# Another cut of the last keys' load, and another place for reordering the last output weights, in a decode attention kernel

## Chip, cores, metric

One core of a Trainium2 chip. The time is the device time of one execution in microseconds. The trace of an execution (its length is called the span) covers some 1.8 us less than the time that is reported for it.

## The reference

Two decode attentions (4 queries) side by side, each with its projections; only the second one, B, matters here, since it streams 537 MB of the 587:

```
q = (x @ wq) as (B=4, H=32, 1, Dh=128);  k, v: (4, 32, 8192, 128) bf16
p = softmax(q k^T / sqrt(Dh));  o = p v;  out_b = o @ wo        (wo: 4096 x 512)
```

## The kernel before

B runs in 64 chunks, each two heads of one batch: 4 MB of keys, 4 MB of values, 128 tiles of 128x128 each. SyncE issues all loads in order: keys of c+1, values of c. Per chunk TensorE transposes the key tiles (groups of 8, into three PSUM tiles in turn, copied out by VectorE or ScalarE), multiplies them with q, and then runs the value matmuls of chunk c-1 with the softmax of chunk c threaded between. Pairs of chunks run in a loop on each engine. The last keys and the last values are loaded in pieces:

```python
LASTV = (64, 32, 16, 8, 8)
...
def dma_kv(kind, c):
    ...
    if kind == "k" and c == NC - 1:
        x = slice(0, NTB // 2 * P), slice(NTB // 2 * P, NTB * P)      # 64 + 64 tiles
        sch.add_dma("sp", lambda e: e.dma_start(dst[:, x[0]], src[:, x[0]]), "d_h%d" % at, waits=waits, key=(kind, c))
        sch.add_dma("sp", lambda e: e.dma_start(dst[:, x[1]], src[:, x[1]]), "d_kl", key="kl")
        return
...
# SyncE counts up when the weights of the pair, and for the last chunk the second key piece, have landed:
sch.add("sp", lambda e: e.sem_inc(sems["eng_sp"], 1), waits=[("wos", hp)] + (["kl"] if c == NC - 1 else []), ...)
...
def emit_T(s):                      # 8 transposes of group g
    ...
    if c >= NCA and c % 2 == 1 and g == NTB // TG // 2:
        waits += [("wos2", ahead(c, 2))]          # the count above
...
sch.mark()                          # after the loop
norm_sum(NC - 1)
emit_wol()                          # 4 matmuls reorder the last output weights, ScalarE and VectorE copy them out
for g in range(chunks[NC - 1]["NG"]):
    emit_pv(NC - 1, g)              # 128 value matmuls; each of the 5 pieces is waited for at its first tile
pv_done(NC - 1)
emit_fin(NC - 1)                    # output matmul, copy, store
```

## Time and profile before

| | before |
|---|---|
| time, first three runs | 1374.6 us (1374.56 to 1375.19) |
| span of the trace | 1373.7 us; its own execution took 1375.56 us |
| load queue busy | 99.7% of the span |
| TensorE (PE) busy | 86% |
| wait for the last value chunk but one, ahead of 1359.14 us | 2.1 us |
| TensorE's granted clock in the 3.41 us behind it | 0.50 |

How to read it: with the load queue busy for 99.7% of the span, I take it that the stream sets the time here, and that the engines add only what they do after its last bytes (the last value piece landed at 1368.99). The granted clock is the share of the full clock that TensorE was given. The lines are in the prediction. Where its stretches of 3.41 us begin is called the phase of the clock; free means not tied to the kernel.

### The profile page before, as it was taken

How to read it: one execution, taken by the hardware profiler on the slowest of the kernel's cores; microseconds unless marked ns; L12 is line 12 of the kernel's file. 1: busy time of each engine (PE TensorE's matmuls, PEld its weight loads, DVE VectorE, ACT ScalarE, POOL GpSimd, SP SyncE). 2: the span in 40 equal slices, each digit the busy share in tenths (PEclk: the TensorE clock that was granted, in tenths of full speed). 3: DMA queues.
4: the chain of work that ended last, by engine and by line, in shares of the span. 5: the costliest groups of instructions: out<-in, count | busy, mean ns of one | idle time of the engine just before them, and what ended most of it. 6: DMA issues, size and time to landing. Idle time of an engine off the chain costs nothing.

```text
span 1373.7 us, 59835 instructions
## 1 busy us (share of the span) xinstructions
PE 1184.8 (86%) x27000; PEld 1134.7 (83%) x27001; DVE 656.5 (48%) x1434; ACT 434.8 (32%) x650; POOL 7.3 (1%) x28
## 2 busy tenths in 40 slices
PE   4898899888889988888889888988888888888988
PEld 4787799888878888888889878988888888888987
DVE  1675455444444544444445444544444444444543
ACT  1553233233323332232333323332332233223332
POOL 2000000000000000000000000000000000000000
PEclk9899999999999999999999999999999999999999
DMA  9999999999999999999999999999999999999998
GB/s 401 423 424 433 426 434 426 437 429 433 429 433 429 432 429 434 428 434 428 434 428 434 429 435 431 431 431 431 431 431 432 430 432 430 432 430 432 430 427 338
DMA packets 25253, 587.53 MB, mean 428 GB/s; under 512 B 2816, under 2 KB 2832, under 8 KB 6288
## 3 DMA queue, kind: packets, MB, share of 16 engines
q1 hardware_dynamic: 25208, 587.22, 99.7%
q8 instruction: 16, 0.26, 0.1%
q14 instruction: 5, 0.04, 0.0%
q10 hardware_dynamic: 24, 0.01, 0.0%
HBM read 587.21 MB, written 0.01 MB: 427 GB/s over the span
## 4 chain that ended last, share of the span: by engine, by line
DMA 59%; PE 37%; DVE 2%; issue 1%; ACT 1%; SPq 0%; DVEq 0%
DMA kv<-in_B_k_cache_dram 54%; PE tr L406 22%; PE sc L408 9%; PE po L408 3%; DMA kv<-in_B_v_cache_dram 2%; DMA kv<-in_B_wq_dram 2%; PE fin L408 2%; DMA kv<-in_A_k_cache_dram 1%; PE ms L408 1%; DVE sA L525 1%; ACT kt L474 0%; DVE rm L534 0%; ACT pba L595 0%; DVE sA L523 0%; PE ms L406 0%
## 5 line engine op out<-in xcount | busy, mean ns | idle before, releaser
L406 PE MATMUL tr<-identb,kv 128*128 128x128 bf16 x8704 | 696.7, 230 | 138.1 <-DMA kv<-in_B_k_cache_dram 133.2
L476 DVE COPY kt<-tr 128x1024 bf16<-128x1024 bf16 x736 | 502.4, 691 | 457.7 <-PE tr L406 453.1
L406 PEld LDWEIGHTS tr<-identb,kv 128*128 128x128 bf16 x8704 | 550.9, 104 | 160.3 <-DMA kv<-in_B_k_cache_dram 91.5
L474 ACT ACTIVATE kt<-tr 128x1024 bf16<-128x1024 bf16 x352 | 359.3, 1023 | 664.9 <-PE tr L406 664.7
L408 PE MATMUL sc<-qb,kt 128*128 128x64 bf16 x8704 | 448.8, 196 | 14.5 <-ACT kt L474 12.8
L408 PEld LDWEIGHTS sc<-qb,kt 128*128 128x128 bf16 x8704 | 368.9, 101 | 25.8 <-ACT kt L474 20.2
L408 PE MATMUL po<-pbb,kv 128*128 128x64 bf16 x8320 | 285.6, 192 | 6.9 <-issue 4.9
L408 PEld LDWEIGHTS po<-pbb,kv 128*128 128x128 bf16 x8320 | 264.8, 97 | 9.3 <-issue 5.1
L575 ACT ACTIVATE pbb<-sc,negb 64x128 bf16<-64x128 f32 x128 | 51.5, 403 | 257.6 <-DVE negb L562 256.9
L539 DVE TENSOR_REDUCE rm<-sc 64x1 f32<-64x128 f32 x128 | 37.0, 289 | 58.9 <-PE sc L408 58.0
L551 DVE TENSOR_REDUCE gm<-ms 1x2 f32<-1x128 f32 (+1 forms) x72 | 20.1, 279 | 48.5 <-PE ms L406 48.5
L562 DVE COPY negb<-ms 128x1 f32<-128x1 f32 (+1 forms) x72 | 11.4, 159 | 47.1 <-PE ms L408 47.1
L408 PE MATMUL ms<-identf,gx 1*128 1x1 f32 (+1 forms) x144 | 27.4, 257 | 0.8 <-DVE zA L681 0.8
L664 DVE TENSOR_TENSOR oz<-po,rz 128x8 bf16<-128x8 f32 x33 | 5.5, 167 | 41.5 <-PE po L408 41.5
L408 PEld LDWEIGHTS ms<-identf,gx 1*128 1x128 f32 (+1 forms) x144 | 21.2, 184 | 4.8 <-DVE zA L681 0.9
L575 ACT ACTIVATION_READ_ACCUMULATOR pbb<-sc,negb 64x1 f32 x128 | 23.7, 185 | 0.0
L406 PE MATMUL ms<-identf,rm 128*1 128x128 f32 (+1 forms) x72 | 19.7, 274 | 4.1 <-DVE rm L534 4.1
L408 PE MATMUL po<-pba,kv 128*128 128x64 bf16 x512 | 20.5, 199 | 2.8 <-issue 1.5
L408 PEld LDWEIGHTS po<-pba,kv 128*128 128x128 bf16 x512 | 17.9, 102 | 5.4 <-ACT pba L595 4.2
L408 PE MATMUL fin<-wos,zB 128*4 128x512 bf16 x64 | 19.0, 378 | 0.0
L555 DVE TENSOR_SCALAR gx<-gm 1x128 f32<-1x128 f32 (+1 forms) x72 | 15.9, 221 | 2.5
L681 DVE CAST zB<-ms 64x8 bf16<-64x8 f32 x64 | 10.5, 164 | 9.4 <-PE ms L408 8.9
(61 smaller groups left out, 169.7 us busy)
## 6 DMA issues: line engine op xcount, KB each, us to landing
kv<-in_B_k_cache_dram SPq DMA_DIRECT2D x63, 4096.0 KB, 26.8
kv<-in_B_v_cache_dram SPq DMA_DIRECT2D x63, 4096.0 KB, 31.2
kv<-in_A_k_cache_dram SPq DMA_DIRECT2D x8, 2048.0 KB, 12.7
kv<-in_A_v_cache_dram SPq DMA_DIRECT2D x8, 2048.0 KB, 14.4
kv<-in_A_wq_dram SPq DMA_DIRECT2D x1, 4096.0 KB, 12.3
kv<-in_B_wq_dram SPq DMA_DIRECT2D x1, 4096.0 KB, 27.2
wor<-in_A_wo_dram SPq DMA_DIRECT2D x8, 512.0 KB, 9.1
wos<-in_B_wo_dram SPq DMA_DIRECT2D x16, 256.0 KB, 20.4
```

What stands on the lines that cost most here:

```text
L406: sch.add("pe", lambda e: e.transpose(o, l, r), waits, key)
L408: sch.add("pe", lambda e: e.matmul(o, l, r, start=start, stop=stop), waits, key)
L474: sch.add("act", lambda e: e.activation(dst, src, ACTF.Copy), waits=waits, key=("ev", s))
L476: sch.add("dve", lambda e: e.tensor_copy(dst, src), waits=waits, key=("ev", s))
L525: emit = lambda e, src=src, b=b: e.scalar_tensor_tensor(out=t, in0=src, scalar=mk[:, b:b + 1], in1=t, op0=ALU.mult, op1=ALU.add)
L539: sch.add("dve", lambda e, src=src, pp=pp: e.tensor_reduce(out=rm[pp, m, 0:1], in_=src, axis=AX.X, op=ALU.max), waits=[("S", ch["s_last"]) ...
L551: sch.add("dve", lambda e: e.tensor_reduce(out=gm[0:C, m, 0:U], in_=src, axis=AX.X, op=ALU.max), waits=[("trm", c)], key=("gmax", c))
L555: sch.add("dve", lambda e: e.tensor_scalar(out=dst, in0=gv, scalar1=-scale, scalar2=None, op0=ALU.mult), waits=[("gmax", c)], key=("gx", c))
L562: sch.add("dve", lambda e: e.tensor_copy(negb[:, m, 0:C], ms[:, col:col + C]), waits=[("bc", c)], key=("negb", c))
L575: sch.add("act", lambda e, src=src, pp=pp, n=n, u=u: e.activation(probs_of(c)[pp, :, u], src, ACTF.Exp, bias=negb[pp, m, 0:1], scale=scale ...
L664: sch.add("dve", lambda e: e.tensor_tensor(out=o, in0=i0, in1=i1, op=ALU.mult), waits=waits, key=("oT", c))
L681: sch.add("dve", lambda e, src=src, pp=pp: e.tensor_copy(z[pp, :].rearrange("p (r b) -> p r b", r=k), src), waits=[("sm", c)] + free if h ...
```

## The change

The intent, as I read it, was to cut the keys so that less work is left behind their last landing, and to use a pause between value pieces for the reordering. Core of the diff:

```diff
+LASTK = 96
-                x = slice(0, NTB // 2 * P), slice(NTB // 2 * P, NTB * P)
+                x = slice(0, LASTK * P), slice(LASTK * P, NTB * P)
-                    if c >= NCA and c % 2 == 1 and g == NTB // TG // 2:
+                    if c >= NCA and c % 2 == 1 and g == LASTK // TG:
                         waits += [("wos2", ahead(c, 2))]
         norm_sum(NC - 1)
-        emit_wol()
         for g in range(chunks[NC - 1]["NG"]):
             emit_pv(NC - 1, g)
+            if g == LASTV[0] // TG - 1:
+                emit_wol()
```

## The prediction

> **What bounds the kernel now.** I read the page first, for the bound of the whole. Its header, engine shares, the three rows of slices and the row of the load queue:
>
> ```profile
> span 1373.7 us, 59835 instructions
> PE 1184.8 (86%) x27000; PEld 1134.7 (83%) x27001; DVE 656.5 (48%) x1434; ACT 434.8 (32%) x650; POOL 7.3 (1%) x28
> DMA  9999999999999999999999999999999999999998
> q1 hardware_dynamic: 25208, 587.22, 99.7%
> ```
>
> The load queue is busy for 99.7% of the span, at 427 GB/s, from the first slice to the last but one. So 587 MB through a full queue set the time, and no saving on an engine in the middle counts. The change touches the last two chunks only (and the place of one wait inside the loop), so I then read the chain of waits over the last 50 us (start, length, what):
>
> ```profile
> 1328.78 30.31 DMA kv<-in_B_v_cache_dram
> 1359.09 0.05 issue
> 1359.14 0.65 PE po L408 x16
> ...
> 1365.36 0.31 PE ms L408 x2
> 1365.68 0.07 issue
> 1365.75 0.81 PE tr L408 x3
> 1366.56 3.76 PE po L408 x128
> ...
> 1371.27 0.68 DVE outsb L716
> ```
>
> The last thing that the chain takes from the queue is the value chunk before the last, landed at 1359.09. From there on it is TensorE alone: the values of that chunk with the last scores between them, the sum (ms), the reordered weights (tr, line 408), the 128 value matmuls of the last chunk, output. Ahead of 1359.14 the list of TensorE's waits has one wait of 2.1 us for that value chunk. Third, the issues of the last key halves in SyncE's timeline, and their time to landing from the views of the two lines (369 and 370):
>
> ```profile
> 1323.43 0.33 SPq L369 DMA_DIRECT2D kv<-in_B_k_cache_dram  x1
> 1323.81 0.43 SPq L370 DMA_DIRECT2D kv<-in_B_k_cache_dram  x1
> DMA to landing us min/median/max: 21.0/21.0/21.0
> DMA to landing us min/median/max: 25.6/25.6/25.6
> ```
>
> The halves land at 1344.4 and 1349.4: 4.9 to 5.0 us for 2 MB, so 2.45 us for 1 MB. TensorE starts on the last keys at 1345.15, directly after the values before them (their last matmul ends at 1345.3): the first half is only 0.7 us early. Last, the busy time of TensorE and its granted clock in stretches of 3.41 us (length, PE, PEld, DVE, ACT, POOL, clock, DMA share, GB/s):
>
> ```profile
> 1352.81:1356.22 3.41, 3.41 (x78) 3.33 (x78) 1.50 (x3) 1.65 (x2) 0.00 (x0) 1.00 0.96 413
> 1356.22:1359.64 3.42, 1.16 (x34) 0.92 (x31) 0.69 (x1) 0.40 (x1) 0.00 (x0) 1.00 0.97 412
> 1359.64:1363.05 3.41, 3.41 (x67) 3.34 (x64) 1.00 (x4) 0.00 (x0) 0.00 (x0) 0.50 0.95 398
> 1363.05:1366.46 3.41, 3.34 (x73) 2.82 (x72) 0.58 (x4) 1.20 (x5) 0.00 (x0) 1.00 0.85 343
> ```
>
> This is the one line that makes the change worth anything: in the stretch with the 2.1 us wait TensorE is busy for 1.16 of 3.42 us, and the next stretch, which lies on the path to the end, runs at half clock. Through the whole trace, going by the clock records, every full-clock stretch of this length with about 1.85 us or more of idle TensorE was followed by one at half clock, and none with under 1.78 us was.
>
> [...] That the phase is free no trace here shows; I take it as a risk. [...]
>
> **The change part by part.**
>
> 1. Keys in 3 MB and 1 MB. The same bytes in the same order: everything from the end of the keys on lands as before (keys 1349.4, values 1359.1). Only the first piece is later by 1 MB, 2.45 us: 1344.4 + 2.45 = 1346.9. TensorE, ready at 1345.3, now waits 1.65 us there. The last keys took from 1345.15 to 1357.08 = 11.9 us; from 1346.95 they end at 1358.9. That is still 0.2 us ahead of 1359.09. So the 2.1 us wait is split: some 1.65 us ahead of the keys, 0.2 us behind them. The first is below the 1.8 us at which half clock followed, the second far below. Then the half-clock stretch at 1359.64 goes. What it cost is read from the same stage one chunk before, at full clock: its values ran from 1340.63 to 1345.31 = 4.68 us; the last such stage from 1359.14 to 1365.36 = 6.22 us. So 1.54 us of TensorE's path are saved.
>
> 2. The wait for the second piece. The listing of instructions shows that the wait for SyncE's count leaves the transposes of group 8 and sits on the output matmul after group 10; the wait meant for group 12 is dropped, since the same value has then been awaited. Before, group 8 began at 1350.92, 1.5 us after the landing at 1349.4, without idle. After, that matmul comes at 1352.37 + 1.8 = 1354.2, 4.8 us after it. No wait before, none after: 0. In the loop the wait moves to a later place; TensorE has 133 us of waiting for keys over the whole kernel, so one more register instruction per two chunks is 0.
>
> 3. Reordered weights between the value matmuls. Four matmuls, 0.9 us of TensorE with the gap before them (1365.68 to 1366.56), come after the first 64 value matmuls. Same work on the same engine. It saves only if a piece of the values is waited for. Before, nothing is: 128 in 3.91 us, 30.5 ns each. After, with part 1: values end at 1363.8, sum to 1364.2 (0.35); piece 1 has landed (1329.2 + 34.8 = 1364.0); 64 matmuls of 30.5 ns to 1366.15; weights to 1367.05; piece 2 (landed at 1366.5) to 1368.0; piece 3 (1367.7) to 1368.5; piece 4 (1368.3) to 1368.75; piece 5 lands at 1331.4 + 37.6 = 1369.0 and is waited for. Eight matmuls and the last one's drain, some 0.45 us: 1369.45. With the weights first, as before, the last matmuls wait for the same piece 5 and end at 1369.45 too. So this part gives 0; the copies of the weights (0.60 and 0.69 us) end by 1368.3, ahead of their use.
>
> The sum: 1370.3 - 1369.45 = 0.85 us, not 1.54, because the landing of the last value piece caps it. What follows the last value matmul (3.4 us to the end of the span) stays. So 1374.6 - 0.85 = 1373.75 if all goes as in this trace. It is 0.06%: nothing near 2%.
>
> **The rivals.**
>
> - *Nothing is gained, because the clock's phase is free.* With a 2.1 us wait, a 3.41 us window may be cut so that neither part holds 1.8 us of idle; I put it at a half at most. Timed runs of before without the half-clock stretch would already end at the cap, and after gains 0. For it: two runs at 1374.56 and 1374.60 and one at 1375.19, a spread of the very size. Against: the two lowest agree within 0.04 us. Time: 1374.6.
> - *The half clock moves instead of going.* If the new wait ahead of the keys is 1.8 us or more within one window, the keys run at half clock for 3.41 us and lose 1.7 us: they end at 1360.6, values at 1365.3, the end as before: 1374.6. A little worse in both: 1375.5. For it: 1.65 is near 1.8. Against: it must also fall whole into one window.
> - *The moved wait disturbs the loop.* Thirty-odd passes; 0.5 us each on the path would be 16 us. Against: the queue is at a share of 1.00 throughout, fed some 20 us ahead, and the wait only moves later. Time then 1380 to 1390; 1%.
> - *The reorder pays of itself*, by filling a wait for value pieces: at most 0.9 us, and only were the pieces later than the sums say. The last piece would still cap it: 1373.7, the same figure.
>
> **Range and chances.** I weigh 1373.75 at two thirds, 1374.6 at one third: 1374.0. Runs of one kernel spread by 0.6 us[...]; 1372.6 to 1375.4 should hold it 8 times in 10. Two per cent is 27 us, and no path above reaches it but a failure of the loop: 0.01 faster, 0.98 within, 0.01 slower.
>
> **What would show it.** Right: the first key piece lands some 2.4 us later, TensorE waits about 1.65 us for keys near 1345.3, the wait for the value chunk at 1359.1 falls under 0.5 us, the clock in the stretch behind it is 1.00, and the last value matmuls wait for the last piece instead of running without a gap. Step 1 is wrong if the clock is 0.50 after 1359 or in the keys; step 2 if a wait for SyncE stands in front of the output matmul; step 3 if the values end earlier than the last piece plus 0.5 us. The whole is wrong if the queue's rate in the middle, 430 to 432 GB/s, differs: then time came or went where I saw no cause.

## The result

Median 1374.43 us (1374.17 to 1374.70, 6 runs), before 1374.58 us (1374.27 to 1375.19, 6 runs). The ratio is 0.9999, 95% interval 0.9986 to 1.0012: the same.

The page after, header and load queue: the stream is as full as before.

```profile
span 1372.9 us, 59836 instructions
q1 hardware_dynamic: 25208, 587.22, 99.7%
```

TensorE's waits from 1340 to 1373 us (waited in total, times, longest), first before, then after:

```profile
PE po L408 <- DMA kv<-in_B_v_cache_dram: 2.1, 1, 2.1
```

```profile
PE tr L407 <- DMA kv<-in_B_k_cache_dram: 1.7, 1, 1.7
PE po L409 <- DMA kv<-in_B_v_cache_dram: 0.5, 2, 0.2
```

The one wait of 2.1 us has become 1.7 us for keys and two of 0.2 us for values. SyncE's two key issues, and their time to landing, after:

```profile
1322.49 0.33 SPq L370 DMA_DIRECT2D kv<-in_B_k_cache_dram  x1
1322.86 0.43 SPq L371 DMA_DIRECT2D kv<-in_B_k_cache_dram  x1
DMA to landing us min/median/max: 24.4/24.4/24.4
DMA to landing us min/median/max: 26.5/26.5/26.5
```

That is 1346.9 and 1349.4: the first piece 2.5 us later than the first half, the whole at the same time. The stretches between changes of the clock, after (columns as in the prediction):

```profile
1344.13:1347.55 3.42, 1.74 (x51) 1.62 (x48) 0.33 (x3) 0.91 (x4) 0.00 (x0) 1.00 1.03 436
1347.55:1350.96 3.41, 3.41 (x79) 3.35 (x77) 2.66 (x4) 1.35 (x2) 0.00 (x0) 1.00 1.07 456
1357.79:1361.20 3.41, 2.98 (x89) 2.73 (x86) 1.27 (x3) 0.67 (x1) 0.00 (x0) 1.00 0.94 399
1361.20:1364.62 3.42, 3.42 (x97) 3.31 (x96) 1.00 (x5) 0.91 (x4) 0.00 (x0) 1.00 0.98 404
```

The clock (third number from the right) is 1.00 in all of them: the half-clock stretch is gone. And the end of the chain of waits, after:

```profile
1330.42 38.58 DMA kv<-in_B_v_cache_dram
1369.00 0.05 issue
1369.04 0.42 PE po L409 x8
```

Before, the chain ended in 12 us of TensorE alone; now it is the load of the last value piece, landed at 1369.00, with eight matmuls behind it. The last value matmul ends 10.35 us after the landing of the value chunk at 1359.1 instead of 11.22; the span is 0.8 us shorter. So the two traces show the whole predicted gain, while the medians differ by 0.15 us, within the noise. That gap is the question for the experiments.

### The profile page after: what moved, and what is told of

Read it like the earlier page. It is cut to its first block, busy times and chain, and to the rows that moved or that the text cites. A ratio compares the mean times of both kernels' runs of the same rounds, so it can differ in the third digit from the quotient of the medians.

```text
span 1372.9 us, 59836 instructions
## 1 busy us (share of the span) xinstructions
PE 1181.3 (86%) x27001; PEld 1131.3 (82%) x27001; DVE 657.2 (48%) x1434; ACT 434.8 (32%) x650; POOL 7.3 (1%) x28
## 3 DMA queue, kind: packets, MB, share of 16 engines
q1 hardware_dynamic: 25208, 587.22, 99.7%
## 4 chain that ended last, share of the span: by engine, by line
DMA 59%; PE 37%; DVE 1%; issue 1%; ACT 1%; SPq 0%; DVEq 0%
DMA kv<-in_B_k_cache_dram 53%; PE tr L407 23%; PE sc L409 9%; DMA kv<-in_B_v_cache_dram 3%; PE po L409 2%; DMA kv<-in_B_wq_dram 2%; PE fin L409 2%; DMA kv<-in_A_k_cache_dram 1%; PE ms L409 1%; DVE sA L526 1%; ACT kt L475 0%; ACT pba L596 0%; DVE rm L535 0%; DVE sA L524 0%; PE ms L407 0%
## 5 line engine op out<-in xcount | busy, mean ns | idle before, releaser
L409 PEld LDWEIGHTS sc<-qb,kt 128*128 128x128 bf16 x8704 | 364.9, 100 | 24.1 <-ACT kt L475 20.3
```

Source lines behind the costliest of these rows:

```text
L409: sch.add("pe", lambda e: e.matmul(o, l, r, start=start, stop=stop), waits, key)
```

## The experiments

The measure for all is local: from the landing of the last value chunk but one (from the chain of waits, or from its load's issue and time to landing) to the end of the last value matmul in TensorE's timeline. It leaves out how the whole stream ran. (Ends of matmuls are modelled by the profile, in all kernels alike.) In the table, "late wait" is TensorE's wait for that value chunk, and the clock is that of the stretch behind it.

| run | keys, first piece | weights | late wait, us | clock behind it | local measure | span | timed runs, us |
|---|---|---|---|---|---|---|---|
| before | 2 MB | first | 2.06 | 0.50 | 11.22 | 1373.7 | 1374.27 to 1375.60 (21) |
| after | 3 MB | between | 0.23 | 1.00 | 10.35 | 1372.9 | 1374.17 to 1374.70 (6) |
| e1_keys_only | 3 MB | first | none | 1.00; 0.50 earlier | 10.76 | 1373.2 | 1374.57 to 1374.98 (4) |
| e2_weights_only | 2 MB | between | 2.06 | 1.00 | 10.36 | 1372.9 | 1374.33 to 1375.25 (4) |
| e3_before_again | 2 MB | first | 2.08 | 0.50 | 11.22 | 1373.6 | 1375.29 (1) |
| e11_before_third | 2 MB | first | 0.50 | 1.00; 0.50 earlier | 10.36 | 1372.9 | 1374.76 (1) |
| e8_after_again | 3 MB | between | 0.24 | 1.00 | 10.36 | 1372.8 | 1374.60 (1) |
| e4_one_piece | 4 MB | between | none | 1.00; 0.50 earlier | 14.05 | 1376.2 | 1377.24 to 1378.43 (4) |
| e6_short_first | 1.5 MB | between | 1.45 | 1.00 | 10.35 | 1372.8 | 1374.57 to 1374.68 (4) |
| e7_no_cap | 3 MB | between | 0.26 | 1.00 | 9.76 | 1372.4 | 1374.11 (1) |
| e9_fill_loop | 2 MB | first | none | 1.00 | 10.36 | 1372.8 | 1374.53 to 1375.20 (4) |
| e10_fill_short | 2 MB | first | 0.69 | 1.00 | 10.29 | 1372.7 | 1374.24 to 1374.45 (4) |

In the traces of before and after, each half clock that ends inside the span lasts 3.41, 6.83, 10.24 or 13.65 us, one to four times 3.41 (windows, below), and where the windows begin, the phase, differs from look to look (half clock from 1359.64 in one look at the kernel before, from 1359.36 in another). Theory: half clock behind the wait makes the path longer, and whether it comes is a matter of the phase; the change shortens the wait; the last landing caps what that is worth. Rival: the change's own moves (the larger first piece, the later reordering) pay.

### e1: the keys alone

```diff
 # the changed kernel, with
         norm_sum(NC - 1)
+        emit_wol()
         for g in range(chunks[NC - 1]["NG"]):
             emit_pv(NC - 1, g)
-            if g == LASTV[0] // TG - 1:
-                emit_wol()
```

> The key pieces of the change alone; the weights are reordered ahead of the value matmuls, as before. Theory (the wait of TensorE is split, so no half clock on the last path; the landing of the last value piece caps the end): the trace is as that of the changed kernel. A wait for keys of about 1.7 us, one for the value chunk of 0.2 to 0.3 us, clock 1.00 after it, 10.3 to 10.4 us from the landing of that value chunk to the end of the last value matmul, span 1372.9. Rival (the reordering pays by filling a wait for value pieces): without it the end comes 0.5 to 0.9 us later, span 1373.4 to 1373.8.

It came out 0.4 us longer than the theory had it, but not by the rival's cause. The stretches:

```profile
1343.50:1346.91 3.41, 1.78 (x49) 1.59 (x46) 0.40 (x3) 0.91 (x4) 0.00 (x0) 1.00 1.00 425
1346.91:1350.32 3.41, 3.41 (x37) 3.41 (x38) 1.38 (x2) 0.63 (x1) 0.00 (x0) 0.50 1.11 473
```

A wait for keys of 1.63 us fell whole into one window, and the keys ran at half clock: the prediction's second rival, come true in one look, at half the cost that it had named (the end 0.4 us later than in the changed kernel, not 0.85). The keys end after the value chunk has landed, and TensorE waits for no load from there on. With nothing waited for, the place of the weights should make no difference, so I put the 0.4 us down to the clock and not to the rival. The other three timed runs of this kernel, 1374.57 to 1374.67, were like the changed kernel's. The timed ratio to before is 0.9996 (0.9980 to 1.0013).

### e2: the place of the reordering alone

```diff
-LASTK = 96
+LASTK = 64
```

> The place of the reordering alone; keys in halves as before. Theory: a wait of 2.1 us for the value chunk, as before. If the window holds 1.8 us of it: half clock after it, 11.2 us from the landing to the last value matmul's end, span 1373.7. If the windows cut it: full clock, 10.4 us, span 1372.9. I give each one half; the two must go together with the clock. Rival (the reordering pays): 10.4 us or less even at half clock.

The wait is 2.06 us as before, but here two windows cut it:

```profile
1354.11:1357.53 3.42, 2.77 (x66) 2.53 (x63) 2.06 (x3) 1.50 (x2) 0.00 (x0) 1.00 1.03 441
1357.53:1360.94 3.41, 1.79 (x61) 1.79 (x62) 0.58 (x2) 0.00 (x0) 0.00 (x0) 1.00 0.91 384
1360.94:1364.35 3.41, 3.41 (x96) 3.27 (x93) 0.83 (x4) 0.91 (x4) 0.00 (x0) 1.00 0.96 398
```

No half clock, 10.36 us, and the chain ends on the last value piece as in the changed kernel, with its eight matmuls from 1369.05. So with keys in halves the end is that of the changed kernel, when the phase is kind. The timed ratio is 0.9997 (0.9981 to 1.0014). By itself this look does not part the reordering from the phase; the third look at the kernel before does. Whether the reordering helps at half clock, as the rival had it, no trace shows; one timed run of this kernel, at 1375.25 us with a span of 1373.5, speaks against it.

### e3 and e11: the kernel before, looked at again

No edit.

> The kernel before, unchanged, for a second look at its last path. Theory (the phase of the clock windows is free of the kernel): the 2.1 us wait is there, and the half clock after it comes in about half of the looks; with it 11.2 us from landing to the last value matmul's end, without it 10.4 us. Rival (the half clock always comes, the phase is fixed): 11.2 us and clock 0.50 again.

> The kernel before, a third look. Theory: wait of 2.1 us for the value chunk; 11.2 us and half clock after it, or 10.4 us and full clock, with even chances; no value between unless the clock changes within the stage.

The first again has the half clock, and 11.22 us:

```profile
1355.95:1359.36 3.41, 1.12 (x31) 0.89 (x29) 0.69 (x1) 0.48 (x1) 0.00 (x0) 1.00 0.96 408
1359.36:1362.77 3.41, 3.41 (x67) 3.34 (x64) 0.81 (x3) 0.00 (x0) 0.00 (x0) 0.50 1.00 424
```

The second has 10.36 us without any edit:

```profile
1329.60:1333.01 3.41, 3.41 (x40) 3.41 (x38) 1.38 (x2) 1.02 (x1) 0.00 (x0) 0.50 0.94 404
1356.91:1360.32 3.41, 2.70 (x76) 2.47 (x74) 1.21 (x3) 1.02 (x1) 0.00 (x0) 1.00 0.97 413
1360.32:1363.74 3.42, 3.42 (x106) 3.33 (x102) 1.00 (x5) 0.91 (x4) 0.00 (x0) 1.00 0.97 407
```

It got there by a road that I had not foreseen: a wait for keys one chunk earlier, 1.86 us here and 0.56 us in the first look, brought half clock at 1329.6, where there is slack. That delayed the keys behind it and ate the later wait down to 0.50 us (my expectation of a 2.1 us wait was wrong). What a stretch at half clock costs depends on the slack behind it: nothing at 1329.6, 0.4 us on the last keys (e1), 0.86 us behind the last wait (11.22 less 10.36).

The same two values show in the timed runs of the kernel before. Sorted, its 21 runs in three sessions fall into eleven at 1374.27 to 1374.68 and ten at 1374.85 to 1375.60. The profiled executions are 1375.56 and 1375.29 with the half clock at the end, and 1374.76, between the groups, without. The spans for 15 of the 21 runs part more clearly: seven at 1372.6 to 1372.9 and eight at 1373.3 to 1373.7, where the traces have 1372.9 without and 1373.6 and 1373.7 with the half clock. That the timed groups are these two cases is still an inference, since timed runs leave no record of where the clock fell.

### e8: the changed kernel again

No edit.

> The changed kernel again, for a second look. Theory: wait for keys of 1.65 us, for the value chunk of 0.2 us; full clock after it, 10.4 us to the last value matmul's end. If a window holds nearly all of the 1.65 us, the keys run at half clock for one window as in the run with the keys alone, and the end is 0.4 us later. Rival: 11.2 us.

As expected: 1.65 us, 0.24 us, full clock, 10.36 us.

### e4: the last keys in one piece

```diff
-LASTK = 96
+LASTK = 128
-            if kind == "k" and c == NC - 1:        # two loads
+            if kind == "k" and c == NC:            # never: one load
-                        waits=[("wos", hp)] + (["kl"] if c == NC - 1 else [])
+                        waits=[("wos", hp)]
```

> The changed kernel with the last keys in one piece of 4 MB, to go past the slack. It lands at the time of the second piece, 4.9 us after the first half of before. Theory: TensorE waits 4.1 us for it, more than a window allows, so the keys run at half clock for one window: they end 1.75 us (late by the slack) + 1.7 us past the landing of the value chunk; 1 to 1.2 us come back, as the values no longer wait for the last piece; the end is 2.5 to 3.5 us later than in the changed kernel. Rival (the clock is of no account): 1.2 to 1.8 us later. Second rival (the first piece's landing is of no account): the same.

Span 1376.2, 3.3 us over the changed kernel, median 1378.06, ratio to before 1.0021 (1.0004 to 1.0037): within the theory's 2.5 to 3.5.

```profile
1343.91:1347.32 3.41, 1.08 (x37) 0.95 (x33) 0.24 (x2) 0.91 (x4) 0.00 (x0) 1.00 1.01 432
1347.32:1354.15 6.83, 5.11 (x57) 5.11 (x58) 2.07 (x3) 1.02 (x1) 0.00 (x0) 0.50 1.00 432
```

A wait of 4.06 us brought two half-clock windows, the first partly over the wait itself. So 3 MB is near the edge: at full clock, the first piece may be some 0.2 us later (the wait that is left for the value chunk) before its landing is on the path to the end; in e1, with the keys at half clock, it was on it already.

### e6: a shorter first piece

```diff
-LASTK = 96
+LASTK = 48
```

> The changed kernel with the last keys cut at 48 tiles (1.5 MB and 2.5 MB) in place of 96. Theory (only how the rest of TensorE is split counts, not a later first piece): no wait for the first piece, about 0.6 us for the second, 1.4 to 1.5 us for the value chunk, so no half clock on the last path; 10.4 us to the end, as in the changed kernel. Rival (a larger first piece is what helps): wait of 2.1 us, clock and end as in the kernel before.

Waits 0.46 us for the second piece and 1.45 us for the value chunk; 10.35 us; full clock. The wait that the change moved is seen at work here, as one for SyncE's count:

```profile
PE po L409 <- DMA kv<-in_B_v_cache_dram: 1.7, 2, 1.4
PE tr L407 <- SPq L398: 0.5, 1, 0.5
```

A smaller first piece ends at the same place as a larger one, so a larger piece is not needed for it. That the split of the wait is what does it, this one look doesn't show: e2 and e11 got there without a split.

### e7: the cap taken away

```diff
-                    x = slice(j0 * P, (j0 + n) * P)
+                    x = slice(j0 * P, (j0 + (n if i == 0 else 1)) * P)
```

> The changed kernel, but the second to fifth value pieces load one tile each (the result is wrong on purpose). Theory: the last landing caps the end, so without it TensorE runs through its 128 value matmuls: 64 of them, the reordering, 64 more from about 1364.05, ending at 1368.9 in place of 1369.45 (9.8 us from the landing of the value chunk before, if the clock is full). Rival (the end is TensorE's own): 10.4 us as before.

The output is wrong, on purpose. TensorE's timeline at the end:

```profile
1364.16 2.05 PE L409 MATMUL po<-pbb,kv 128*128 128x64 bf16 x64
1366.06 1.02 PE L409 MATMUL tr<-wos,back 128*128 128x512 bf16 x4
1366.92 2.04 PE L409 MATMUL po<-pbb,kv 128*128 128x64 bf16 x64
```

No pause, 9.76 us instead of 10.36 (9.8 expected). So in this one look 0.6 us of TensorE's saving is hidden by the last landing in the changed kernel; that was the cap.

### e5: filling the wait, a failed try

```diff
                 emit_S(late[0])
+                if nxt == NC - 1:
+                    for _ in range(48):
+                        pe_mm(tr[:, 1, :].bitcast(F32)[:, 0:NW], identb[:, :], identb[:, 0:NW])
```

> The kernel before with 48 idle matmuls (to a free bank, result unused) put between the last scores and the last but one value chunk, so that TensorE does not rest for more than about 0.6 us there; the last pair of chunks leaves the loop by this. Theory: no half clock after the landing of the value chunk, in whatever phase; 10.4 us from the landing to the last value matmul's end, span 1372.9, that is, all that the changed kernel has, without its change. Rival (it is the place of the pieces and of the reordering that pays, not the clock): 11.2 us as in the kernel before. All timed runs should lie in the lower group of before's runs (1374.3 to 1374.7), none at 1375.0 to 1375.4.

4 us slower: span 1377.3, ratio 1.0031 (1.0015 to 1.0048). The edit took the last pair of chunks out of TensorE's loop, so that it became straight code. TensorE's waits from 1340 us, and the row of instruction loads of this kernel, which is 16 packets and 0.26 MB in the kernel before:

```profile
PE po L408 <- issue: 2.2, 2, 1.4
PE ms L408 <- issue: 1.9, 1, 1.9
```

```profile
q8 instruction: 22, 0.36, 0.1%
```

Three waits of 1.87, 1.40 and 0.84 us have no engine and no data load as their end, and six more instruction packets, 0.10 MB, went over the DMA engines; the load view of the last 37 us has six (0.10 MB). Whether the waits are for these packets was not shown, and I did not test it; e9, with the same matmuls and the loop whole, has no such wait, so the broken loop goes with them. As a test of the clock this run says nothing.

### e9: filling the wait, with the loop whole

```diff
+                if (nxt - NCA) % 2 == 1:          # in every pair of chunks; rest as in e5
```

> The fill again, mended: in the run before, the last pair of chunks had left the loop and TensorE waited 1.9, 1.4 and 0.8 us for no engine and no load [...]. Here the 48 idle matmuls stand in every second pass's scores, so that the loop stays whole; they cost 1.5 us of TensorE in 39 us, in a place where it waits anyway. Otherwise the kernel before, keys in halves, weights first. Theory: wait for the value chunk 0.6 us, no half clock after it, 10.4 us from its landing to the last value matmul's end, span 1372.9, all timed runs in the lower group (1374.3 to 1374.7), with no part of the change in it. Rival (the place of the pieces pays, not the clock): 11.2 us, half of the runs at 1375.0 to 1375.6.

The trace is the theory's, but for the 0.6 us that I expected of the wait: none for the value chunk, only 0.2 us for the last piece, full clock, 10.36 us.

```profile
PE po L408 <- DMA kv<-in_B_v_cache_dram: 0.2, 1, 0.2
```

Keys in halves, weights first: nothing of the change is in it, and in the trace it has all of the change's gain. Two of its four timed runs, at 1374.79 and 1375.20, missed the range that I expected (1374.3 to 1374.7), and the second has a span of 1373.4, like the upper group. They left no trace; why is open.

### e10: the fill, and a shorter last piece

```diff
-LASTV = (64, 32, 16, 8, 8)
+LASTV = (64, 32, 16, 12, 4)                       # on e9
```

> The same with the last two value pieces of 12 and 4 tiles in place of 8 and 8. Theory: after the last landing four matmuls are left in place of eight, 0.12 us less: 10.2 to 10.3 us from the landing of the value chunk to the last value matmul's end; span 1372.7 to 1372.8. It is the quickest that the theory offers by these means, and 0.1 us will not show in the timed runs. Rival: the fourth piece of 12, landing later, is waited for in its turn and the gain is lost: 10.4 us.

10.29 us, within the expected range but only about half of the 0.12 us hoped for: the fourth piece, now larger, is waited for in its turn, 0.27 us, and the last four matmuls follow its twelve without a wait (16 in one stretch from 1368.66). In the kernel before, the value pieces of 1, 0.5, 0.25 and 0.25 MiB landed 2.47, 1.24, 0.64 and 0.64 us after the one ahead of them, so at 424, 423, 409 and 412 GB/s.

```profile
1368.66 0.64 PE L408 MATMUL po<-pbb,kv 128*128 128x64 bf16 x16 [0.27 <-DMA kv<-in_B_v_cache_dram]
```

Its runs, 1374.24 to 1374.45, are low throughout, but the ratio to before is 0.9994 (0.9978 to 1.0011): not shown to beat either kernel.

## Why the prediction was right, and where it was off

**The bound** held: 99.7% of the load queue before and after, and every trace that left the loop whole had a span of 1372.4 to 1376.2 us.

**Step 1, the keys.** Landing 1346.9, wait 1.65 us, keys' end 1358.9, rest of the wait 0.2 us: measured 1346.9, 1.68, 1358.92 and 0.23. The half clock was gone in both looks at the changed kernel. Its size, 1.54 us of TensorE capped to 0.85, was measured as 0.87 (11.22 less 10.35) in the local measure; without the cap it was 1.46 (11.22 less e7's 9.76), so the cap is the last landing. Two things were off. The bound of 1.8 us of idle time ahead of half clock came from one trace (2.26 us in 3.42 ahead of the stretch at 1359.64) and does not hold in others: 1.63 us was followed by half clock in e1, 1.68 us in the changed kernel and 1.62 us in e2 were not. Idle time alone does not tell these apart. And the place of the gain: it is not due to a larger piece as such, since 1.5 MB did as well (e6), and an idle fill too (e9).

A count over the kept traces, made afterwards, parts the windows better. For each window of 3.41 us at full clock (by the clock records of the trace), add up, for the matmuls that start in it, the columns that each streams (the last figure of its shape in the timeline: 128 for a transpose, 64 for a matmul of scores or values). In the kernel before, each of its windows with 3072 columns or fewer was followed by half clock and none with 3136 or more was. A cut between the two, at 3104, misplaces 7 of the 4519 such windows of all thirteen traces; the best cut by idle time, 1.85 us, misplaces 47. The windows of this argument: before 1728 columns, e3 1664, e4 1984 and e1 2626, each followed by half clock; changed kernel 3520 and 3648 (e8), e2 3904 and e6 3136, none followed. (Of the 7, one is e11's at 1326.19: 3136, and followed; another is the changed kernel's at 794.59: 3010, and not followed.) The window of e1 held value matmuls ahead of its wait and no transpose; that of the changed kernel, cut 0.6 us later, held some 11 transposes behind it, each worth two value matmuls in this count. These are counts over these traces; what sets the clock they do not show, and no experiment was made to test it.

**Step 2, the moved wait**: no wait for SyncE in the changed kernel, and the queue's rate in the loop (900 to 1018 us) is 431 GB/s, where it was 430 to 432. Right.

**Step 3, the reordering**: 0, right. The kernel before with weights first and full clock takes 10.36 us (e11), with the reordering between 10.36 (e2).

**The rivals.** The first, that the phase is free and before often has nothing to lose, is what held the medians together: of three looks at the kernel before, two had half clock at the end and one did not, and its timed runs lie in two groups of eleven and ten. The second came true in e1, with a shorter wait than it had named (1.63 us, not 1.8) and at half its cost. The one third that it gave the first was too low, by the groups: eleven of 21 runs of the kernel before have nothing to lose.

**The step that failed, inside the range,** is "So 1374.6 - 0.85 = 1373.75 if all goes as in this trace", weighed at two thirds. I took the saving read in one execution from the median of others. The traced execution of before took 1375.56 us, one of the upper group; 1375.56 less 0.87 is 1374.69, and the traced execution of after took 1374.70. The median of before, 1374.58, is that of six runs of which four lie in the lower group and had nothing to gain. Before's mean less after's mean of the six runs each is 0.19 us, and that is within the interval. The range, 1372.6 to 1375.4, holds "no change" as well as the forecast gain, so a time inside it does not tell the two apart.

What the change does to the timed runs shows best in how often they are long. Of the 15 runs with the keys cut elsewhere than in halves and loaded in two pieces (after, e1, e6, e8), one is above 1374.70, the traced run of e1 at 1374.98; of the 21 of the kernel before, ten are. (With the keys in halves and other edits, e2 has one of four, e9 two of four, e10 none of four.) This, too, was counted afterwards, and over more than one chip and session; no ratio shows the change to be faster.

## What to carry to other kernels

A saving read in a trace belongs to the execution that was traced: subtract it from that execution's own time, and look at the kernel two or three times before deciding that a clock dip or a wait in its tail is part of it. When a full load queue sets the time (99.7% busy here), work out what lands last and what must follow it; here the tail gained only up to that landing (0.87 us, and 1.46 with the landing out of the way). Ask also what a wait brings: one of 2.06 us went with 10.36 us in e2, at full clock behind it, and with 11.22 us in the kernel before, at half clock behind it. An experiment must leave the loop structure alone: taking one pass out of a loop went with 4 us (e5), more than any effect studied here.
